# Longer load times in a kernel's own planner: the second batch's folds move back in GpSimd's order

## The chip, the cores and the metric

The kernel runs on one core of one Trainium2 chip. The metric is the device time of one execution in microseconds. A core has five engines that each work through their own instruction stream in order: TensorE (matmuls; PE in the profile, with its weight loads as PEld), VectorE (DVE), ScalarE (ACT), GpSimd (POOL) and SyncE (SP), which here only issues DMAs.

## The reference

A Fourier mixing step on 8 batches of 3008 rows with 256 columns, of which the real part is kept, and then a SwiGLU feed-forward layer on all 24064 rows:

```python
X = np.fft.fft(x, axis=1); X = np.fft.fft(X, axis=2)     # x: 8 x 3008 x 256
x = X.real.astype(np.float32).reshape(24064, 256)
g = x @ w_gate                                           # w_gate, w_val: 256 x 1536
val = x @ w_val
out = (g / (1 + np.exp(-g))) * val @ w_out               # w_out: 1536 x 256
```

## The kernel before

**The work.** The transform along the rows is a product with cosine and sine tables, and symmetry lets one half of the output rows carry the other (their mirror image). The transform along the columns is folded into the weights. The output columns of the eight half transforms, 8 times 1504, are cut into 24 tiles: 480 + 512 + 512 for the first batch, the same for the second, and 512 from there on. A tile has twelve units, one for each block of 128 hidden features; units are counted through all tiles, so unit 33 is the tenth of the third tile.

**A unit.** TensorE makes the gate `g` and the value `v` from the tile's even part `Pt` and odd part `Qt` (all at L1346). ScalarE and VectorE turn them into the gated product of the row, `hp` (L1560), and into the two factors of the mirror row, `sv` (ScalarE at L1533, VectorE at L1549). A buffer of `sv` holds the factors of two units, and there are two such buffers. GpSimd multiplies the factors of a pair of units: `hm` (L1557), 1024 elements in a partition. In some units GpSimd also makes `hp` (L1566), from a copy `pp` of the value (ScalarE, L1563). Until `hm` of a pair is done its `sv` buffer isn't free, and the pair after the next cannot be written. A tile later TensorE multiplies `hp` and `hm` with `w_out` (`o`, L1608), ScalarE evicts `ev`, and SyncE stores it (L1620).

**The folds.** Before the row transform of a batch, its rows are loaded (tile `XA` for the greater part, `XC` for the rest) and folded on GpSimd into sums and differences. One fold is six steps: `cross` (L189, L190), `even` (L193), `odd` (L196), `ab` (L199), `ce` (L202, L203) and `bb` (L211 to L213). The first step waits for all loads of its tile. The second batch has one fold of `XC` (into `Fc`, which SyncE spreads into `St`, L1735) and two folds of `XA` (into `CEa` and `BBa`). Small copies on GpSimd put one column of these aside (`Z`, L1877 and L1879). From `CEa`, `St` and `Z` TensorE makes the transform (`o` and `g`, L1766 and L605); ScalarE copies `od` out (L1773), and VectorE writes `Pt` and `Qt` with sums and differences (`puts`, L1783 and L1789). `sel` (L1937) is the first matmul of a tile that reads its `Qt`.

**The order.** All this is not written out in order. A planner in the kernel (class `Sched`) is told of each operation: its engine, a duration, what it reads and writes, and a due time, the plan's TensorE time plus a shift that a table gives for its kind and tile. `run` then deals the operations out greedily: for each engine it looks in a window of due times for the one that can begin first, and the engine's stream gets the order that comes out. Durations are guesses that set this order and nothing else: each instruction on the chip still waits for what it truly needs. A load has two numbers: `us`, how long SyncE is taken by it, and `ring`, how much later it lands than the load before. In `run`:

```python
if o.eng == "SP":
    ring = max(o.end + o.lat, ring + o.ring)
    o.lat = ring - o.end
    lanes = lanes[1:] + [ring]
```

With `lanes` no load starts until the eighth before it has landed. The loads of the second batch are listed in `run_loads` (L1669 on): `("C", 1)` are those of `XC`, 25 of them, and `("A", 1)` those of `XA`, 20, in the orders `C1_ORDER` and `A1_ORDER`, where `u` stands for blocks of rising rows and the other letters for sets of falling rows and a copy. `S.run({...})` at L2006 begins the plan; its numbers say how long after TensorE each engine is first free.

Of the kernel before, what the change touches and what calls it, by code (L numbers as in the profile page):

```python
# [31 lines left out]
def kernel(  # L32
# [113 lines left out]
    C1_ORDER = "uuduuduuduuduumuueuueuece"  # L146
    A1_ORDER = "uuuuduuuuduuuuduuuud"
# [1200 lines left out]
    S = Sched()  # L1348
# [307 lines left out]
    for b in range(2, B, 2):  # L1656
        u = slot[(b, 0)] - 1
# [11 lines left out]
    def run_loads(n):  # L1669
        for what, k, fn in loads[:n]:  # L1670
            up = k < (NA if what[0] == "A" else NC_)
            r, w, us, ring = [], [((what[0],), k)], 0.4 if up else 0.62, 0.57 if up or what[0] == "C" else 1.14
            if what == ("A", 1):
                r = [(("C",), C1_ORDER.rindex("u"))]
                us, ring = (0.35, 0.5) if A1_ORDER[k] == "u" else (0.65, 0.9)
            if what == ("C", 1):
                us, ring = (0.35, 0.45) if C1_ORDER[k] == "u" else (0.85, 0.75)
                if C1_ORDER[k] == "c":
                    r = [(("C",), j) for j, o in enumerate(C1_ORDER) if o == "u"]
            S.add("SP", us, fn, r=r, w=w, after=[(("A",), "pre" if A1_ORDER[k] == "d" else "preW")] if what == ("A", 1) else [],  # L1680
                  lat=2.5, ring=ring)
        del loads[:n]
# [4 lines left out]
    def fold_step(what, i, unit):  # L1687
        kind, b = what
        q, j = (1, i) if what == ("C", 1) else divmod(i, 6)
        if i == 0:  # L1690
            run_loads(max((k + 1 for k, (w_, _, _) in enumerate(loads) if w_ == what), default=0))
# [105 lines left out]
    for b, part in jobs[1:]:  # L1797
        for eo in range(2):
            u = slot[(b, part)] + eo
# [156 lines left out]
    for i, u in enumerate(units):  # L1956
# [6 lines left out]
        if i == A1_LOAD:  # L1963
            loads[0:0] = ((("A", 1), k, fn) for k, fn in enumerate(load_a(1, nc.sync)))
        run_loads(LOADS if i < 20 else LOADS_LATER)
        if i in ROW_PE:
            row_op(ROW_PE[i])
# [35 lines left out]
    part_b(prev)  # L2003
    owork = OWork(prev[0], ((psG, "g"), (psV, "v"), (psO, "o")))
    owork.run(len(owork.steps))
    S.run({'DVE': 1.2, 'ACT': 0.9, 'POOL': 3.5, 'PE': 0.0, 'SP': 1.0})  # L2006


# [28 lines left out]
```

## Time and profile before

| | |
|---|---|
| median of 3 runs | 607.98 us (607.45 to 609.18) |
| the profiled execution | 607.87 us |
| its span, from the first to the last instruction | 606.1 us |
| mean granted TensorE clock | 0.997 |
| GpSimd busy | 509.7 us, 460 instructions |
| VectorE busy | 571.4 us, 1055 instructions |
| ScalarE busy | 562.8 us, 1086 instructions |

A row of the timeline gives the start, the length, the engine, the line, the operation, the written and the read tile, and how many instructions were merged; in square brackets stands how long the engine had been idle and what ended that. A row of the windows gives for each engine the busy time and, in brackets, how many instructions, then the granted clock of TensorE (1.00 is full speed), the DMA engines' busy share and GB/s.

### The profile page before, as it was taken

To read this page: it belongs to the slowest core of one execution; us is meant where nothing else is said; L and a number is where in the kernel's file an instruction comes from. 1 tells how busy PE (TensorE), PEld (TensorE's weight loads), DVE (VectorE), ACT (ScalarE), POOL (GpSimd) and SP (SyncE) were. 2 spreads that over 40 slices of the span, in tenths; PEclk is the share of its full clock that TensorE was granted. 3 is DMA by queue.
4 is the path that set the end of the run, shared out by engine and by line. 5 is a ranking of instruction groups with operands and counts; after the bars stand their busy time and mean duration, and the time that the engine had idled before them with its cause. 6 is when DMAs were issued, how large, how long until landed. Compare 5 with 4: busy or idle time off the path is not lost.

```text
span 606.1 us, 12508 instructions
## 1 busy us (share of the span) xinstructions
PE 592.5 (98%) x3974; PEld 392.2 (65%) x4031; DVE 571.4 (94%) x1055; ACT 562.8 (93%) x1086; POOL 509.7 (84%) x460
## 2 busy tenths in 40 slices
PE   8999899999999999999999999999999999999997
PEld 5556566666666666666666666666666666666685
DVE  8989699999999999999999999999999999999993
ACT  8999798899989899999999999999999999999994
POOL 9737998999799999998999988887878467687772
PEclk9999899999999999999999999999999999999999
DMA  9846347254616214454136212036211112111112
GB/s 240 142 106 136 113 118 182 65 141 114 185 39 166 80 55 121 121 130 129 55 82 142 66 45 81 18 94 179 63 62 37 57 43 66 42 54 51 54 53 79
DMA packets 50555, 57.65 MB, mean 95 GB/s; under 512 B 7267, under 2 KB 37399, under 8 KB 50489
## 3 DMA queue, kind: packets, MB, share of 16 engines
q1 hardware_dynamic: 47529, 53.97, 32.8%
q0 software_dynamic: 2672, 2.36, 2.7%
q8 instruction: 31, 0.51, 0.4%
q10 hardware_dynamic: 288, 0.52, 0.3%
q14 instruction: 35, 0.29, 0.2%
HBM read 29.43 MB, written 24.65 MB: 89 GB/s over the span
## 4 chain that ended last, share of the span: by engine, by line
PE 88%; DMA 5%; ACT 2%; issue 1%; DVE 1%; POOL 1%; SPq 1%; DVEq 0%; ACTq 0%
PE o L1608 38%; PE g L1346 24%; PE v L1346 19%; DMA XA<-in_x_dram 3%; DMA XC<-in_x_dram 2%; PE g L1766 2%; PE o L1766 2%; PE v L1608 1%; PE o L1814 0%; POOL SDf L189 0%; ACT sp L1458 0%; PE o L605 0%; PE g L605 0%; POOL hm L1557 0%; ACT sv L1533 0%
## 5 line engine op out<-in xcount | busy, mean ns | idle before, releaser
L1557 POOL TENSOR_TENSOR hm<-sv 128x1024 bf16<-128x1024 f32 (+2 forms) x137 | 254.8, 1861 | 52.2 <-ACT sv L1533 24.0
L1549 DVE SCALAR_TENSOR_TENSOR sv<-es,v 128x512 f32<-128x512 f32 (+2 forms) x264 | 175.8, 670 | 9.3 <-PE v L1346 4.8
L1608 PE MATMUL o<-Wo,hm 128*128 128x256 bf16 (+1 forms) x1128 | 164.8, 274 | 0.4
L1560 DVE TENSOR_TENSOR hp<-sp,v 128x512 bf16<-128x512 f32 (+2 forms) x238 | 157.9, 670 | 5.0 <-PE v L1346 3.6
L1608 PE MATMUL o<-Wo,hp 128*128 128x256 bf16 (+1 forms) x1104 | 160.2, 272 | 0.7
L1608 PEld LDWEIGHTS <-hm 128*128 128x128 bf16 (+2 forms) x1140 | 112.6, 99 | 59.6 <-issue 3.3
L1608 PEld LDWEIGHTS <-hp 128*128 128x128 bf16 (+2 forms) x1140 | 111.9, 98 | 56.0 <-issue 1.8
L1533 ACT ACTIVATE sv<-g 128x512 f32<-128x512 f32 (+2 forms) x182 | 120.8, 678 | 5.6 <-POOL hm L1557 2.8
L1458 ACT ACTIVATE sp<-g 128x512 f32<-128x512 f32 (+2 forms) x182 | 113.5, 626 | 5.9 <-PE g L1346 3.2
L1346 PE MATMUL g<-Pt,Wp 128*128 128x512 bf16 (+2 forms) x282 | 105.8, 375 | 3.7 <-ACT sv L1533 2.7
L1419 ACT ACTIVATE v<-bc,w 128x512 f32<-128x512 bf16 (+2 forms) x146 | 105.4, 724 | 2.0 <-DVE sv L1549 1.0
L1346 PE MATMUL v<-Pt,Wp 128*128 128x512 bf16 (+2 forms) x287 | 105.3, 375 | 0.5
L1483 DVE SCALAR_TENSOR_TENSOR es<-bc,w,v 128x512 f32<-128x512 bf16 (+2 forms) x128 | 93.3, 732 | 2.7 <-PE v L1346 0.4
L1481 ACT ACTIVATE es<-v 128x512 f32<-128x512 f32 (+2 forms) x146 | 90.5, 622 | 5.6 <-DVE sv L1549 2.7
L1346 PE MATMUL g<-Qt,Wq 128*128 128x512 bf16 (+2 forms) x246 | 90.3, 374 | 0.3
L1346 PE MATMUL g<-Qt,Wm 128*128 128x512 bf16 (+2 forms) x192 | 72.1, 377 | 0.9 <-ACT sg L1381 0.5
L1346 PEld LDWEIGHTS <-Wp 128*128 128x128 bf16 x576 | 56.4, 98 | 25.1 <-issue 0.8
L1462 DVE SCALAR_TENSOR_TENSOR sg<-bc,w,g 128x512 f32<-128x512 bf16 (+2 forms) x92 | 66.2, 722 | 1.9 <-PE g L1346 1.5
L1533 ACT ACTIVATE sv<-sg 128x512 f32<-128x512 f32 (+2 forms) x92 | 64.0, 699 | 1.0 <-DVE sg L1526 0.9
L1530 ACT ACTIVATE sp<-g 128x512 f32<-128x512 f32 (+2 forms) x92 | 56.9, 618 | 5.3 <-DVE sg L1526 5.1
L1346 PEld LDWEIGHTS <-Wq 128*128 128x128 bf16 x430 | 42.0, 98 | 30.4 <-issue 6.4
L1526 DVE SCALAR_TENSOR_TENSOR sg<-sg,g 128x512 f32<-128x512 f32 (+2 forms) x92 | 60.7, 660 | 0.1
(196 smaller groups left out, 768.8 us busy)
## 6 DMA issues: line engine op xcount, KB each, us to landing
out_dram<-ev SPq DMA_DIRECT2D x96, 128.0 KB
XA<-in_x_dram SPq DMA_DIRECT2D x30, 256.0 KB
XA<-in_x_dram SPq DMA_DIRECT2D x112, 64.0 KB
XC<-in_x_dram SPq DMA_DIRECT2D x28, 120.0 KB
XC<-in_x_dram SPq DMA_DIRECT2D x105, 32.0 KB
bc<-br SPq DMA_DIRECT2D x19, 128.0 KB
St<-Fc SPq DMA_DIRECT2D x12, 128.5 KB
out_dram<-ev SPq DMA_DIRECT2D x12, 120.0 KB
```

What stands on the lines that cost most here:

```text
L1346: nc.tensor.matmul(ps[:, :n], Wt[:, gv, fs], src[:, :n], start=start, stop=stop, skip_group_check=True)
L1419: nc.scalar.activation(T_[kv][:, :w], bc[t][:, :w], AF.Copy, scale=w0[:, 1, f:f + 1])
L1458: nc.scalar.activation(sp_to()[:, :w], T_[kg][:, :w], AF.Silu)
L1462: nc.vector.scalar_tensor_tensor(T_[keg][:, :w], bc[t][:, :w], w0[:, 0, f:f + 1], T_[kg][:, :w], op0=Alu.mult, op1=Alu.add)
L1481: nc.scalar.activation(T_[kes][:, :w], T_[kv][:, :w], AF.Copy, scale=2.0 if on_pool(u) > 1 else 1.0)
L1483: nc.vector.scalar_tensor_tensor(T_[kes][:, :w], bc[t][:, :w], w0[:, 1, f:f + 1], T_[kv][:, :w], op0=Alu.mult, op1=Alu.add)
L1526: nc.vector.scalar_tensor_tensor(T_[kgm][:, :w], T_[keg][:, :w], 2.0, T_[kg][:, :w], op0=Alu.mult, op1=Alu.subtract)
L1533: nc.scalar.activation(sv()[:, f % 2, w - 1::-1, 1], T_[kgm if by_dve else kg][:, :w], AF.Silu)
L1549: nc.vector.scalar_tensor_tensor(sv()[:, f % 2, w - 1::-1, 0], T_[kes][:, :w], 2.0, T_[kv][:, :w], op0=Alu.mult, op1=Alu.subtract)
L1557: nc.gpsimd.tensor_tensor(hts_(t)[1][:, f - 1:f + 1, :w], sv()[:, :, :w, 1], sv()[:, :, :w, 0], op=Alu.mult)
L1560: nc.vector.tensor_tensor(hts_(t)[0][:, f, :wp], T_[ksp][:, :wp], T_[kv][:, :wp], op=Alu.mult)
L1608: nc.tensor.matmul(st["ps"][:n, j, :], hts[t][minus][:, f, c:c + n], Wo[:, f, :], start=(f == 0), stop=(f == nF - 1))
```

## The change

Two lines of planned load times and the line that begins the plan:

```diff
             if what == ("A", 1):
                 r = [(("C",), C1_ORDER.rindex("u"))]
-                us, ring = (0.35, 0.5) if A1_ORDER[k] == "u" else (0.65, 0.9)
+                us, ring = (0.35, 0.65) if A1_ORDER[k] == "u" else (0.65, 1.0)
             if what == ("C", 1):
-                us, ring = (0.35, 0.45) if C1_ORDER[k] == "u" else (0.85, 0.75)
+                us, ring = (0.45, 0.66) if C1_ORDER[k] == "u" else (0.9, 0.92)
...
-    S.run({'DVE': 1.2, 'ACT': 0.9, 'POOL': 3.5, 'PE': 0.0, 'SP': 1.0})
+    S.run({'DVE': 1.6, 'ACT': 1.2, 'POOL': 3.3, 'PE': 0.0, 'SP': 1.0})
```

No instruction is added, removed or changed; what comes out is another order. Around the fold of `XC` and the first fold of `XA`, GpSimd's order was and becomes (in parentheses the units of the second tile, counted from 0):

```
before                            after
XC: cross even odd ab bb ce       XC: cross even odd ab bb
hm (0,1)                          hp (1)
hp (1)                            hm (0,1)
XA: cross even odd                XC: ce
hm (4,5)                          hm (4,5)
hm (6,7)                          XA: cross
XA: ab bb ce                      hm (6,7)
hm (8,9)                          XA: even odd
hm (10,11)                        hm (8,9)
XA second fold: cross even        hm (10,11)
hm (third tile: 0,1)              XA: ab bb ce
...                               hm (third tile: 0,1)
                                  XA second fold: cross
```

Through this stretch the order of ScalarE, VectorE and TensorE is the same in both. They differ in two places: in the first tiles (some table builds and weight copies change places, `Wo`'s load comes one instruction earlier on GpSimd), and from the second batch's transform on, whose products stand 25 matmuls of 256 or 512 columns later in TensorE's order, its first `puts` three instructions later in VectorE's. On SyncE three stores of the first tile move ahead of eight loads of the next `XC`. From the fifth tile on the orders differ only by a few exchanged neighbours, and from the eleventh tile on not at all.

## The prediction

> **What bounds the kernel now.** First the page's busy times, then the windows of 20 us around the second batch's folds (columns: stretch, its length, busy PE, PEld, DVE, ACT, POOL, PEclk, DMA share, GB/s):
>
> ```profile
> span 606.1 us, 12508 instructions
> PE 592.5 (98%) x3974; PEld 392.2 (65%) x4031; DVE 571.4 (94%) x1055; ACT 562.8 (93%) x1086; POOL 509.7 (84%) x460
> ```
>
> ```profile
> 40.00:60.00 20.00, 19.86 (x128) 12.69 (x128) 19.38 (x33) 18.32 (x35) 12.77 (x13) 1.00 0.65 133
> 60.00:80.00 20.00, 17.17 (x106) 11.48 (x107) 15.02 (x25) 16.15 (x32) 19.92 (x19) 0.91 0.40 111
> 80.00:100.00 20.00, 19.89 (x136) 13.14 (x137) 20.00 (x42) 17.86 (x35) 17.00 (x17) 1.00 0.62 144
> ```
>
> TensorE is the bound: whatever makes it wait or run slowly is lost, and nothing else counts. Only 13.6 us of the span are left for that. The window from 60 us on sticks out: 17.17 us busy, 106 instructions against 128 and 136 in the windows beside it, and a clock of 0.91. So I read GpSimd's timeline there; ahead of it stands TensorE's longest wait of the whole run, from the view of waits (total, times, longest).
>
> ```profile
> PE g L1346 <- ACT sv L1533: 2.7, 1, 2.7
> ```
>
> ```profile
> 50.09 0.20 POOL L213 TENSOR_TENSOR Fc<-EOf 128x2 bf16<-128x2 f32 x1
> 50.84 0.64 POOL L203 TENSOR_TENSOR Fc<-Af 128x258 bf16<-128x258 f32 x1
> 51.44 1.89 POOL L1557 TENSOR_TENSOR hm<-sv 128x1024 bf16<-128x1024 f32 x1
> 53.29 1.28 POOL L1566 TENSOR_TENSOR hp<-sp,pp 128x512 bf16<-128x512 f32 x1
> 58.59 2.35 POOL L189 TENSOR_TENSOR SDf<-XA 128x1020 f32<-128x1020 f32 x1 [4.03 <-DMA XC<-in_x_dram]
> 63.16 3.74 POOL L1557 TENSOR_TENSOR hm<-sv 128x1024 bf16<-128x1024 f32 x2
> 66.86 1.10 POOL L199 TENSOR_TENSOR Af<-EOf 128x516 f32<-128x516 f32 x1
> 70.58 3.75 POOL L1557 TENSOR_TENSOR hm<-sv 128x1024 bf16<-128x1024 f32 x2
> ```
>
> GpSimd stands idle for 4.03 us at the head of the first `XA` fold, because the rows have not landed, and two `hm` of the second tile (units 4,5 and 6,7) stand behind the fold's first 4.57 us. Who waits for them:
>
> ```profile
> 56.74 0.68 ACT L1533 ACTIVATE sv<-g 128x512 f32<-128x512 f32 x1
> 65.08 0.64 ACT L1533 ACTIVATE sv<-g 128x512 f32<-128x512 f32 x1 [2.84 <-POOL hm L1557]
> 68.57 0.64 ACT L1533 ACTIVATE sv<-g 128x512 f32<-128x512 f32 x1
> 65.08 0.69 DVE L1549 SCALAR_TENSOR_TENSOR sv<-es,v 128x512 f32<-128x512 f32 x1 [3.74 <-POOL hm L1557]
> 62.51 0.60 PE L1608 MATMUL o<-Wo,hm 128*128 128x256 bf16 x4
> 65.77 0.38 PE L1346 MATMUL g<-Pt,Wp 128*128 128x512 bf16 x1 [2.67 <-ACT sv L1533]
> 65.98 0.38 PE L1346 MATMUL g<-Qt,Wq 128*128 128x512 bf16 x1
> ```
>
> Both `sv` buffers are full until the `hm` of units 4,5 ends at 63.16 + 1.87 = 65.03. At 65.08 ScalarE and VectorE go on with unit 8, and 0.7 us later TensorE, which had a gate buffer held by it. After that the clock falls:
>
> ```profile
> 65.77:70.27 4.50, 4.44 (x18) 2.90 (x18) 4.01 (x8) 3.80 (x7) 4.42 (x7) 0.62 0.49 139
> 70.27:74.77 4.50, 4.50 (x32) 3.03 (x31) 4.34 (x8) 4.30 (x9) 4.50 (x4) 1.00 0.39 104
> ```
>
> 18 matmuls in 4.50 us at a granted clock of 0.62, where the next 4.50 us hold 32.
>
> **Part 1: the stall goes.** In the changed order TensorE, ScalarE and VectorE do the same in the same order through this stretch; GpSimd alone is rearranged: `hp`, `hm` (0,1) and the `hm` of (4,5) come ahead of the `XA` fold, and `hm` (6,7) after its `cross`. I walk GpSimd with the rows' lengths:
>
> ```profile
> 50.37 0.56 ACT L1563 COPY pp<-v 128x512 f32<-128x512 f32 x1
> 53.16 0.54 SPq L153 DMA_DIRECT2D XA<-in_x_dram  x1
> 53.81 4.76 SPq L166 DMA_DIRECT2D XC<-in_x_dram  x8
> ```
>
> The `XC` fold starts when its loads land, as before. `hp` now stands at 50.29 and waits for `pp` (50.93), so 51.0 to 52.3; `hm` (0,1) to 54.1; `ce` (1.25) to 55.4. `hm` (4,5) waits for the `sv` of unit 5, which ScalarE ends at 56.74 + 0.68 = 57.42: 57.45 to 59.32. That frees its buffer 5.7 us earlier than before. The `XA` rows land at 58.59 at the latest. Their last load is issued at 53.16, and nothing ahead of it on SyncE moves; behind it three stores of 256 KB together replace eight loads of as much. So `cross` runs 59.32 to 61.8 without a wait, `hm` (6,7) to 63.7. Unit 8 wants its buffer at 62.2, when ScalarE is free (65.08 less 2.84), and has it 2.9 us before. Unit 10 followed unit 8 by 3.49 us (68.57, half of it at the low clock); at full pace it wants the other buffer some 2.5 to 3.5 us after 62.2, a microsecond or two after 63.7. No wait is left.
>
> What this gives: TensorE's gap, from 62.51 + 0.44 (four products of 256 columns at half of the 0.216 us between 65.77 and 65.98 each, 0.109) = 62.95 to 65.77, is 2.82 us. The slow stretch holds 6 matmuls of 512 columns and 12 of 256: 6 x 0.216 + 12 x 0.109 = 2.60 us at full clock, against 4.50, so 1.90 more. Gross gain 4.72 us. A cross-check: 106 instructions instead of some 132 (the mean of the neighbours) at 0.15 us each is 3.9 us.
>
> [...]
>
> **Part 2: what comes next late.** GpSimd regains less than TensorE, for it still loses time: 0.7 us at `hp` and 2.1 us before `hm` (4,5). From 57.45 on it does in a row what it did from 58.59 on, so it is 1.1 us ahead, while the others are 4.7 ahead. The places where it is read next:
>
> ```profile
> 84.36 0.63 POOL L203 TENSOR_TENSOR CEa<-Af 128x258 bf16<-128x258 f32 x1
> 88.25 0.20 POOL L1879 COPY Z<-CEa 128x4 bf16<-128x4 bf16 x1
> 89.04 1.89 POOL L1557 TENSOR_TENSOR hm<-sv 128x1024 bf16<-128x1024 f32 x1 [0.59 <-ACT sv L1533]
> 93.27 1.89 POOL L1557 TENSOR_TENSOR hm<-sv 128x1024 bf16<-128x1024 f32 x1 [2.33 <-DVE sv L1549]
> 95.12 2.36 POOL L189 TENSOR_TENSOR SDf<-XC 128x1020 f32<-128x1020 f32 x1
> 87.63 0.33 PE L1766 MATMUL g<-Tab,CEa 128*128 128x189 bf16 x2
> 90.99 0.49 PE L605 MATMUL o<-Tab,Z 128*128 128x189 bf16 x3
> 94.58 0.37 PE L1937 MATMUL g<-Qt,sel 128*128 128x480 bf16 x1
> 91.76 0.51 ACT L1773 COPY od<-o 128x377 f32<-128x377 f32 x1
> 93.04 1.19 DVE L1783 TENSOR_TENSOR Qt<-g,od 128x188 bf16<-128x188 f32 x5
> 94.15 0.15 DVE L1789 TENSOR_TENSOR Qt<-g,od 128x1 bf16<-128x1 f32 x1
> 84.16 0.63 SPq L168 DMA_DIRECT2D XC<-in_x_dram  x1
> ```
>
> *`CEa`.* Before it was done at 84.99, after 26.40 us of GpSimd without a pause since 58.59. Now one more `hm` (units 4,5 of the third tile, 1.87) stands ahead: 57.45 + 26.40 + 1.87 = 85.7. TensorE's first product with it now has 5 matmuls of 512 and 20 of 256 columns more ahead, 3.26 us: 87.63 + 3.26 - 4.72 = 86.2. Reached with 0.5 us to spare. `Z` is ready 1.6 us after `CEa` (`bb`, which is 88.25 less 84.99 less the `hm` between them, 1.4, and the copy, 0.20), at 87.3, and TensorE wants it 1.6 us after its first product (a `g` and five matmuls), at 87.8. Reached with 0.5. Cost 0; if GpSimd is late by more, up to 0.7 us.
>
> *The third tile's end to the fourth tile's `Qt`.* The last transform product now is an `o`, after which the ScalarE copy (0.51) and six `puts` (1.26) are due before `sel`; with three handoffs of some 0.2 us (an estimate, from the 0.28 us between the last `put`, which ends at 94.30, and `sel` at 94.58) that is 2.4 us. Behind that `o` TensorE has 7 matmuls of about 512 columns and 8 of 256, 2.36 us. No margin: 0 if both engines are free at that moment, up to 1.4 us if each has one instruction of 0.7 us ahead. I take 0.4.
>
> *The `sv` buffers of the third and fourth tile.* GpSimd frees them. It idled for 0.59 and 2.33 us ahead of 89.04 and 93.27; that it can take up, which makes it 1.1 + 2.9 = 4.0 us ahead from there on at best, the others 4.3. Where the margin was smaller than the difference, a bit is lost: 0 to 0.6, taken as 0.2.
>
> *The first 45 us.* Table builds and copies change places.
>
> ```profile
> 34.62 0.51 ACT L1895 ACTIVATE St<-EOf,sgn 128x256 bf16<-128x256 bf16 x1
> 35.52 0.48 PE L1766 MATMUL o<-Tab,BBa 128*128 128x376 bf16 x2
> ```
>
> The copy at 34.62 (0.51) stood behind the last sine table and now stands ahead of it, and the first product that reads the tables came 0.9 us after the sine's end. Between the sine and that product VectorE still scales the table. So 0.1, from -0.3 to 0.4.
>
> *The next `XC` fold.* It comes forward to 95.12 - 4.0 = 91.1. The last load in front is issued by 84.79; the last `XA` load took 58.59 - 53.70 = 4.89 us from its issue, so 89.7. Hidden by 1.4 us.
>
> Behind that all orders are alike up to a few neighbours, and every load waits for a fold or store that comes as much earlier. Sum: 4.72 - 0.4 - 0.2 - 0.1 = 4.0 us. Against the profiled execution, 607.87 (its span 606.1 and 1.77 around it), that is 603.9; that execution lies 0.1 below the median of the three runs, 607.98.
>
> **The rivals.**
>
> *GpSimd stays the bound* (0.16). Its lead, 1.1 growing to 4.0 us, rather than TensorE's 4.7 sets the pace from 60 to 125 us, and `CEa`, `sel` and a buffer each cost their upper bound: 4.72 - 0.7 - 1.4 - 0.6 = 2.0, with the first 45 us 1.6 to 2.3. Time 605.9. For it: GpSimd was 19.92 us busy of 20 from 60 us on. Against: it idles 3 us at 80 to 100 us, where it can catch up.
>
> *The slow clock has another cause* (0.06). Then the 4.50 us at 0.62 come without the gap too, and the gain is 2.82 - 0.7 = 2.1, time 605.8. [...]
>
> *The wait moves to another load* (0.08, slower than before). GpSimd meets the next `XC` fold earlier. If the rows land after 95 us, the fold holds up GpSimd with `hm` (10,11) of the third tile behind, just as the `XA` fold did. A wait of 6 us there would cost TensorE some 4.8 us and 1.9 us of half clock: 6.7 - 4.0 = 2.7 slower, 610.6. It decides from a landing 10 us after the issue on, against the 4.89 us seen: unlikely.
>
> *It doesn't do what it says* (0.08). The `XA` rows land later with the stores behind them or the first stage shifts, and a stall of nearly the same size stays: 607.0, from 606.3 to 607.9.
>
> **How the numbers follow.** The forecast (603.9; 603.0 to 605.0 by its bounds) has 0.62. Differences of 0.3%, 1.8 us, are about what a measurement of this kernel can tell from no change. Faster by more than that (below 606.1): forecast 0.62, and two thirds of the two smaller gains, 0.15; together 0.77. Same: the rest of these and the last rival, 0.15. Slower: 0.08. The range takes in the smaller gains: 602.8 to 606.4.
>
> **What would show it.** In the changed profile, GpSimd's first `XA` `cross` should have no DMA wait or less than 0.5 us, and stand behind three `hm`/`hp` of the second tile; the waits of ScalarE and VectorE for `hm` should be gone, the window from 60 to 80 us should hold some 132 TensorE instructions at a clock of 1.00, and the windows after 100 us should be as before, 4 us earlier. It would be wrong if TensorE showed a wait of over a microsecond at `CEa` or `sel`, if the clock fell again anywhere, or if a fold waited for rows.

## The result and the profile after

The changed kernel takes 603.47 us (median of 6 runs, 603.0 to 603.94), against 607.87 for the kernel before in runs beside it (6 runs, 607.45 to 609.8). The ratio is 0.9921, with a 95% interval of 0.9905 to 0.9936: faster by 4.4 us. The profiled execution took 603.29 us, 1.8 of it around the span.

The busy times of the page, and the same three windows as before (busy PE, PEld, DVE, ACT, POOL, then PEclk, DMA share, GB/s):

```profile
span 601.5 us, 12495 instructions
PE 590.3 (98%) x3974; PEld 390.5 (65%) x4031; DVE 572.5 (95%) x1055; ACT 562.5 (94%) x1086; POOL 510.1 (85%) x460
```

```profile
40.00:60.00 20.00, 19.86 (x129) 12.78 (x129) 19.39 (x34) 18.33 (x34) 13.70 (x14) 1.00 0.65 140
60.00:80.00 20.00, 19.84 (x135) 13.39 (x137) 19.54 (x32) 20.00 (x41) 19.92 (x18) 1.00 0.40 107
80.00:100.00 20.00, 19.95 (x140) 13.29 (x139) 19.57 (x42) 16.16 (x32) 19.82 (x20) 1.00 0.62 157
```

The middle window has gone from 106 TensorE instructions to 135 and from a clock of 0.91 to 1.00. GpSimd is as busy there as it was, 19.92 us, but in the third window it has 19.82 instead of 17.00: it does the same work sooner. Its timeline through the changed stretch:

```profile
51.22 1.27 POOL L1566 TENSOR_TENSOR hp<-sp,pp 128x512 bf16<-128x512 f32 x1 [0.51 <-PE v L1346]
52.45 1.89 POOL L1557 TENSOR_TENSOR hm<-sv 128x1024 bf16<-128x1024 f32 x1
54.91 0.64 POOL L203 TENSOR_TENSOR Fc<-Af 128x258 bf16<-128x258 f32 x1
57.72 1.89 POOL L1557 TENSOR_TENSOR hm<-sv 128x1024 bf16<-128x1024 f32 x1 [2.18 <-ACT sv L1533]
59.57 2.36 POOL L189 TENSOR_TENSOR SDf<-XA 128x1020 f32<-128x1020 f32 x1
62.04 1.90 POOL L1557 TENSOR_TENSOR hm<-sv 128x1024 bf16<-128x1024 f32 x1
65.98 3.75 POOL L1557 TENSOR_TENSOR hm<-sv 128x1024 bf16<-128x1024 f32 x2
...
85.32 0.64 POOL L203 TENSOR_TENSOR CEa<-Af 128x258 bf16<-128x258 f32 x1
87.37 0.20 POOL L1879 COPY Z<-CEa 128x4 bf16<-128x4 bf16 x1
91.22 2.35 POOL L189 TENSOR_TENSOR SDf<-XC 128x1020 f32<-128x1020 f32 x1
```

The `XA` cross at 59.57 has no bracket: GpSimd spends the time until the rows land on the `hm` of units 4,5 and waits for nothing afterwards. Units 8 and 10 find their `sv` buffers free (ScalarE's timeline, no brackets):

```profile
62.34 0.64 ACT L1533 ACTIVATE sv<-g 128x512 f32<-128x512 f32 x1
65.29 0.71 ACT L1533 ACTIVATE sv<-g 128x512 f32<-128x512 f32 x1
```

TensorE reaches the three places that the prediction feared without a bracket, here in its timeline, and its longest waits of the whole run are now elsewhere (view of waits); all four were there in before, where the one for the first `XA` rows was 0.6 us shorter:

```profile
86.47 0.33 PE L1766 MATMUL o<-Tab,CEa 128*128 128x189 bf16 x2
88.10 0.49 PE L605 MATMUL g<-Tab,Z 128*128 128x189 bf16 x3
91.44 0.37 PE L1937 MATMUL g<-Qt,sel 128*128 128x480 bf16 x1
```

```profile
PE o L310 <- DVE sel L261: 1.0, 1, 1.0
PE v L497 <- ACT EOb L512: 1.0, 2, 0.8
PE g L444 <- DMA XA<-in_x_dram: 0.8, 1, 0.8
PE g L1346 <- ACT sp L1530: 0.7, 1, 0.7
```

**Where the time comes from** is seen when TensorE's timelines of the two kernels are laid side by side, matmul by matmul: the start in before less the start after is TensorE's lead. One place serves as an example, the gate product behind the slow stretch, first of before, then of after:

```profile
70.27 0.38 PE L1346 MATMUL g<-Qt,Wm 128*128 128x512 bf16 x1
```

```profile
65.76 0.38 PE L1346 MATMUL g<-Qt,Wm 128*128 128x512 bf16 x1
```

The lead is -0.21 us up to before's 62.51, 4.51 at 70.27, 4.40 still at 150, 4.59 at 168, 4.38 at 590. The whole gain, 4.72 us, arises within 8 us, and little of it is given back.

### The profile page after: what moved, and what is told of

Its sections match the earlier page's. It is cut to its first block, busy times and chain, and to the rows that moved or that the text cites. A ratio compares the mean times of both kernels' runs of the same rounds, so it can differ in the third digit from the quotient of the medians.

```text
span 601.5 us, 12495 instructions
## 1 busy us (share of the span) xinstructions
PE 590.3 (98%) x3974; PEld 390.5 (65%) x4031; DVE 572.5 (95%) x1055; ACT 562.5 (94%) x1086; POOL 510.1 (85%) x460
## 4 chain that ended last, share of the span: by engine, by line
PE 90%; ACT 3%; DVE 2%; issue 2%; DMA 2%; POOL 1%; SPq 0%; ACTq 0%; DVEq 0%
PE o L1608 39%; PE g L1346 24%; PE v L1346 20%; PE g L1766 2%; PE o L1766 2%; DMA XA<-in_x_dram 1%; PE v L1608 1%; DVE sv L1549 1%; ACT sp L1458 1%; ACT sv L1533 1%; PE o L1814 1%; POOL EOA L511 0%; ACT v L1419 0%; PE g L605 0%; DVE es L1483 0%
## 5 line engine op out<-in xcount | busy, mean ns | idle before, releaser
L1346 PE MATMUL v<-Qt,Wm 128*128 128x512 bf16 (+2 forms) x158 | 59.0, 374 | 0.6
```

Source lines behind the costliest of these rows:

```text
L1346: nc.tensor.matmul(ps[:, :n], Wt[:, gv, fs], src[:, :n], start=start, stop=stop, skip_group_check=True)
```

## Experiments

Two theories. Theory 1: GpSimd has no time to spare from 58 to 88 us, so the stall is only where its lateness first shows; take it away there, and it comes back at the next place that needs GpSimd. Theory 2: the one wait for rows, with the `hm` behind it, is everything.

Experiments 1 to 4 take the kernel before and move operations in GpSimd's stream alone, after the planning. All other engines keep before's order. Their edit is a helper that is called in `run`'s last loop:

```diff
+def rearranged(order):
+    pool = [o for o in order if o.eng == "POOL"]
+    for move, at, after in (((15, 16, 17), 18, 1),):
+        move, at = [pool[k] for k in move], pool[at]
+        order = [o for o in order if o not in move]
+        i = order.index(at) + after
+        order[i:i] = move
+    return order
...
-            for o in order:
+            for o in rearranged(order):
```

The numbers count GpSimd's operations in before's order: 15, 16, 17 are `cross`, `even` and `odd` of the first `XA` fold, 18 and 19 the `hm` of units 4,5 and 6,7, 20 to 22 the fold's last three steps, 24 the `hm` of units 10,11; from 25 on follow the second `XA` fold and the third tile's `hm`. The lead columns of the table below are worked out as above, from rows of the timelines.

**Experiment 1, e1_hm_first**: `((15, 16, 17), 18, 1)`, the fold's first three steps behind the `hm` of units 4,5.

> The kernel before with one exchange on GpSimd: the hm of units 4,5 of the second tile ahead of the first three steps of the XA fold (cross, even, odd); all other engines keep their order. Theory 1 (GpSimd has no time to spare from 58 to 88 us: every hm there frees an sv buffer that is wanted at once, and the folds stand between them): the stall at unit 8 goes, but GpSimd is only 1.1 us ahead of before (57.45 instead of 58.59), so new waits of ScalarE and VectorE for hm come up at the third tile's units 0, 6 and 8, where before there was 0.9, 0.5 and 0.05 us of margin. Gain 1.1 to 1.2 us, 606.7. Theory 2 (one stall, behind one wait for rows, is all there is): the whole gain, 603.5.

607.25 us, ratio 0.9982 [0.9974, 0.9991]. TensorE's timeline, and two lines of its waits view (50 to 130 us):

```profile
65.87 0.38 PE L1346 MATMUL g<-Qt,Wm 128*128 128x512 bf16 x1
...
67.42 0.38 PE L1346 MATMUL v<-Pt,Wp 128*128 128x512 bf16 x1 [0.52 <-ACT v L1419]
73.13 0.38 PE L1346 MATMUL g<-Qt,Wq 128*128 128x512 bf16 x1 [0.22 <-DVE sg L1462]
74.23 0.38 PE L1346 MATMUL g<-Pt,Wp 128*128 128x512 bf16 x1 [0.52 <-ACT sv L1533]
84.20 0.38 PE L1346 MATMUL g<-Qt,Wm 128*128 128x512 bf16 x1 [0.74 <-ACT sp L1458]
88.24 0.38 PE L1346 MATMUL g<-Pt,Wp 128*128 128x512 bf16 x1 [0.40 <-ACT sv L1533]
...
93.80 0.37 PE L1937 MATMUL g<-Qt,sel 128*128 128x480 bf16 x1
```

```profile
DVE sv L1549 <- POOL hm L1557: 2.4, 2, 1.8
ACT sv L1533 <- POOL hm L1557: 2.4, 3, 1.1
```

The big wait and the low clock are gone, and at the product that begins at 70.27 in before TensorE leads by 4.40. Then five waits, each for ScalarE or VectorE, whose own longest waits are for `hm`, take most of it back: 2.4 us in the brackets, and some 0.16 more at each, as a row of 0.38 us ends later than the next product can begin (0.22 us on). With smaller gaps that no bracket shows, the lead at `sel` is 0.78. Theory 2 falls.

**Experiment 2, e2_one_step**: `((16, 17), 18, 1)`, only `even` and `odd` behind that `hm`; `cross` with its wait stays in front.

> The kernel before with the hm of units 4,5 of the second tile behind the first step (cross) of the XA fold instead of behind three; GpSimd still waits for the rows at 58.59. Theory 1: the stall at unit 8 shrinks from 2.8 us to some 0.8 and the clock stays at 1.00 there, but GpSimd's work up to 88 us ends when it did before, and the third tile's unit 8, whose buffer came free 0.05 us before it was wanted, now waits for it: gain 0.0 to 0.3 us, 607.7. Theory 2: the stall is shorter by 2.1 us and the half clock (1.9) gone: gain 4.0, 603.9. For the clock: if a gap of under a microsecond leaves it at 1.00, the 2.82 us were what lowered it.

607.75 us, 0.9990 [0.9981, 0.9999]. The row wait of 3.64 us is still there, but the clock never falls (1.00 in every window); TensorE's lead at 70.27 is 3.88, and 0.27 at `sel`. So before's wait for rows costs little by itself: nearly the same wait, with one step instead of three between it and the `hm`, gives 4.17 of the 4.72 at first and loses most of it likewise. Experiment 1, which has no such wait, ends 0.5 us sooner.

**Experiment 3, e3_stretch**: `((15,), 18, 1), ((16, 17), 19, 1), ((20, 21, 22), 24, 1)`, the changed kernel's order on GpSimd up to the first fold's end.

> The kernel before with GpSimd's order of the changed kernel in the second tile alone: hm 4,5, cross, hm 6,7, even, odd, hm 8,9, hm 10,11, ab, bb, ce; from the second XA fold on as before, and all other engines as before. Theory 1: no wait within the second tile, but in the third, where the fold's steps still stand ahead of hm as before and GpSimd is 1.1 us ahead only: gain 1.2 us, 606.7. Theory 2: 603.5.

607.32 us, 0.9983 [0.9974, 0.9992]. The windows and the later of TensorE's waits:

```profile
60.00:80.00 20.00, 20.00 (x136) 13.37 (x135) 19.53 (x32) 19.14 (x39) 19.92 (x19) 1.00 0.40 113
80.00:100.00 20.00, 17.10 (x116) 11.01 (x115) 16.92 (x37) 15.16 (x30) 17.03 (x17) 1.00 0.58 156
```

```profile
80.62 0.38 PE L1346 MATMUL g<-Qt,Wm 128*128 128x512 bf16 x1 [0.55 <-ACT sp L1458]
84.67 0.38 PE L1346 MATMUL g<-Qt,Wm 128*128 128x512 bf16 x1 [1.94 <-ACT sp L1458]
88.72 0.38 PE L1346 MATMUL g<-Pt,Wp 128*128 128x512 bf16 x1 [0.42 <-ACT sv L1533]
```

Here the first 20 us are without any loss, TensorE busy for 20.00 of 20.00, and the second 20 have it instead. The stall has moved to the third tile's `sv` buffers, behind the second `XA` fold, which is still where it was.

**Experiment 4, e4_gpsimd_all**: experiment 3 and `((25,), 27, 1), ((26, 28), 31, 1), ((30, 29, 32, 33), 34, 1)`, so that GpSimd has the changed kernel's order through the second fold too. TensorE's transform stays where it was.

> The kernel before with GpSimd's order of the changed kernel from the XA fold to the end of the third tile's folds; TensorE, ScalarE and VectorE keep the order of before, in which the second batch's transform stands 25 matmuls earlier. Theory 1: no sv wait, but CEa is ready at 86.0 and TensorE wants it at 83.2: a TensorE wait of up to 2.8 us at L1766, which may halve the clock once more (1.9 us): gain 0 to 1.7, 606.2 to 607.9. Theory 2 (GpSimd's order is all that matters): 603.5.

608.09 us, 0.9994 [0.9985, 1.0004]: no gain at all. TensorE's timeline:

```profile
85.43 0.26 PE L1766 MATMUL g<-Tab,CEa 128*128 128x189 bf16 x1 [2.01 <-POOL CEa L202]
86.03 0.26 PE L1766 MATMUL g<-Tab,CEa 128*128 128x188 bf16 x1 [0.34 <-POOL CEa L203]
```

Now no `sv` buffer is late, and `CEa` is: it is written at 84.74 and 85.34, where before's TensorE, 4.5 us ahead, wants it from 83.4 on. Behind this gap the clock falls again, to 0.50 from 86.80 to 90.00 us (last section). The four runs in one table:

| lead over before, us | TensorE at 62.51 | at 70.27 | at `sel`, 94.58 | GpSimd at `Z`, 88.25 |
|---|---|---|---|---|
| e2_one_step | -0.29 | 3.88 | 0.27 | 0.27 |
| e1_hm_first | -0.32 | 4.40 | 0.78 | 0.79 |
| e3_stretch | -0.79 | 3.94 | 0.30 | 0.31 |
| e4_gpsimd_all | -0.25 | 4.47 | 0.00 | 0.87 |

The first column is what the first 60 us happened to differ by. From it to the second column, each but e2 gains 4.72 or 4.73. By `sel` TensorE's lead has shrunk, in three of four to GpSimd's own within 0.01 us; over the stretch, experiments 1 and 3 keep 1.1 us, which is the 1.1 that the prediction's walk gave GpSimd. In the fourth, `CEa` comes later in GpSimd's order and takes the rest as well.

**Experiment 5, e5_loads_only**, and **6, e6_begin_only**: the change without its third line, and that line alone.

```diff
 # e6_begin_only; e5_loads_only is the other two lines
-    S.run({'DVE': 1.2, 'ACT': 0.9, 'POOL': 3.5, 'PE': 0.0, 'SP': 1.0})
+    S.run({'DVE': 1.6, 'ACT': 1.2, 'POOL': 3.3, 'PE': 0.0, 'SP': 1.0})
```

> The change without its last line: the longer load times, with the plan begun as before. The order of the first tiles is then that of before, and all the rest that of the changed kernel. Theory 1: the whole gain, 603.5. Rival (the exchanges in the first tiles matter): 0.3 us or more beside 603.5.

> The last line of the change alone: the plan begun with other times. Only the first tiles' order changes (table builds, weight copies, one load). Theory 1: nothing, 607.9, within 0.3. Rival: up to a microsecond either way.

The loads alone give 602.51 us, 0.9911 [0.9897, 0.9925]: all of the gain. The last line alone gives 607.26, 0.9986 [0.9978, 0.9995], 0.8 us that I had not expected. GpSimd's and TensorE's timelines show the old stall, smaller:

```profile
57.95 2.36 POOL L189 TENSOR_TENSOR SDf<-XA 128x1020 f32<-128x1020 f32 x1 [3.50 <-DMA XC<-in_x_dram]
65.14 0.38 PE L1346 MATMUL g<-Pt,Wp 128*128 128x512 bf16 x1 [1.98 <-ACT sv L1533]
```

The rows landed 0.64 us earlier than in before (57.95 against 58.59), `Z` comes 0.66 earlier (87.59) and `sel` 0.64 (93.94). Again GpSimd's lead is TensorE's. Why the rows landed earlier I did not test. Whether it adds anything to the change was the next question.

**Experiments 9, e9_change_again, and 10, e10_loads_again**: the change and experiment 5, side by side.

> The changed kernel once more, for a comparison on one chip with the next one: 0.9921 of before, 603.3. Theory 1 as it stands: the first tiles' order is worth nothing in the changed kernel, so this and the next are equal within 0.3 us. Rival: the next is faster by 0.6 us or more, and the change's last line costs that.

> The longer load times without the change's last line, beside the changed kernel on one chip. Theory 1: equal within 0.3 us. Rival: faster by 0.6 us or more (602.5 against 603.5, as the medians of two different chips stand).

603.29 us, 0.9924 [0.9911, 0.9938], and 603.02, 0.9921 [0.9908, 0.9935]. The two can't be told apart: the third line does nothing for the changed kernel that these runs show, and none of them points to a version that beats it.

**Experiments 11, e11_xa_only, and 12, e12_xc_only**: one of the two load lines each.

```diff
 # e11_xa_only
-                us, ring = (0.35, 0.5) if A1_ORDER[k] == "u" else (0.65, 0.9)
+                us, ring = (0.35, 0.65) if A1_ORDER[k] == "u" else (0.65, 1.0)
 # e12_xc_only
-                us, ring = (0.35, 0.45) if C1_ORDER[k] == "u" else (0.85, 0.75)
+                us, ring = (0.45, 0.66) if C1_ORDER[k] == "u" else (0.9, 0.92)
```

> The longer times for the XA loads alone. In GpSimd's order cross and even of the XA fold then still stand ahead of the hm of units 4,5. Theory 1: the stall at unit 8 shrinks to 1.8 us, and GpSimd's work up to 88 us ends when it did before: gain 0.0 to 0.6, 607.5. Theory 2 (later folds are better, by as much as they are later): half the gain, 605.8.

> The longer times for the XC loads alone. cross of the XA fold stands ahead of the hm of units 4,5. Theory 1: a stall of 0.8 us at unit 8, GpSimd at most 0.4 us ahead of before at 88 us: gain 0.3 to 0.9, 607.3. Theory 2: half the gain or more, 605.8 or less.

`XA` alone: 607.65 us, 0.9997 [0.9988, 1.0006]. TensorE waits at both of the places that experiments 1 to 4 separated, at the second tile's gate and in the third tile:

```profile
64.83 0.38 PE L1346 MATMUL g<-Pt,Wp 128*128 128x512 bf16 x1 [1.13 <-ACT sv L1533]
85.21 0.38 PE L1346 MATMUL g<-Qt,Wm 128*128 128x512 bf16 x1 [1.45 <-ACT sp L1458]
```

`XC` alone: 608.69, 1.0014 [1.0005, 1.0023], a miss, for I had expected a small gain. Up to 135 us it has one: the lead goes from -0.93 at 62.51 to 1.03. It is lost after that, in a tile that this order arranges otherwise; the window from 140 us on, of this kernel and of after:

```profile
140.00:160.00 20.00, 17.59 (x112) 10.50 (x113) 16.73 (x34) 18.20 (x37) 18.52 (x18) 1.00 0.54 130
```

```profile
140.00:160.00 20.00, 19.13 (x126) 12.27 (x128) 18.60 (x39) 20.00 (x40) 17.64 (x18) 1.00 0.55 144
```

At 160 us the lead is -2.05. A load time that is told to the planner moves everything behind it, not only what it was meant for; here that costs 3 us, 80 us later.

**Experiment 7, e7_cross_first**: the changed kernel, with one step set back, `((16,), 15, 0)` (numbers of the changed order): the `XA` cross again ahead of the `hm` of units 4,5.

> The changed kernel with one exchange: the XA fold's cross ahead of the hm of units 4,5 again, so that GpSimd waits for the rows first. Theory 1: unit 8 waits 0.8 us for its buffer, GpSimd is 1.1 us later from there on, TensorE waits some 0.5 us at CEa, where the changed kernel has 0.5 us of margin, and loses 0.7 to 1.2 us in all: 604.2 to 604.7. Theory 2 (the wait for the rows is the cause): the gain goes back to a half or less, 605.5 or more.

603.97 us, 0.9936 [0.9923, 0.9948]. GpSimd waits for the rows again:

```profile
57.69 2.36 POOL L189 TENSOR_TENSOR SDf<-XA 128x1020 f32<-128x1020 f32 x1 [2.54 <-DMA XA<-in_x_dram]
```

VectorE then waits 0.9 us for an `hm`. TensorE has no wait that the view shows singly, only small gaps from 62 to 68 us; against after it is 0.38 us ahead at 54 and 0.27 behind at 102, so the step costs 0.65 us. A wait of 2.54 us on GpSimd that costs 0.65: theory 1's figure nearly (the rows landed 0.9 us earlier than in before), and far from a return of the 4.4.

**Experiment 8, e8_six_steps**: before, with the stall made longer, `((20, 21, 22), 18, 0)`: all six steps of the fold ahead of the `hm` of units 4,5.

> The kernel before with the hm of units 4,5 of the second tile behind all six steps of the first XA fold: GpSimd frees the buffer 3.72 us later. Both theories: TensorE's gap grows from 2.8 to 6.5 us, time 611.6. For the clock: if the half clock after the gap lasts as long as it did behind 2.82 us (3.4 us), its price is fixed once it falls; if it grows with the gap, more than 612.

612.28 us, 1.0074 [1.0059, 1.0088]. TensorE's timeline:

```profile
68.81 0.59 PE L1346 MATMUL g<-Pt,Wp 128*128 128x512 bf16 x1 [5.52 <-ACT sv L1533]
```

The wait grows from 2.67 to 5.52 us, and the time at half clock from 3.4 to 6.8 us, of which matmuls run for 5.3 (last section). What is placed ahead of that `hm` is paid for at TensorE, in full and more.

## Why the prediction was right

**The bound and the stall.** The gross term, 2.82 us of gap and 1.90 of half clock, 4.72, is what TensorE gains in after, in experiment 1 and in experiment 3 between before's 62.51 and 70.27 (4.51 + 0.21, 4.40 + 0.32, 3.94 + 0.79). But the half clock is a loss of the profiled execution rather than of the kernel. Of the 21 executions of before beside experiments 9 to 12, nine have a mean clock of 0.997 or less, as one such fall makes it (3.4 us at 0.50 in a span of 606.1), and take 608.09 us on average; the other twelve have 0.998 or more, too high for a fall, and take 607.92. Beside experiments 1 to 8 the difference is 0.3 to 0.4 us, not 1.9. No trace of an execution of before without the fall was kept, but experiment 2 shows where the time can go: there the clock stays up, and what TensorE gains is lost in waiting further on. The changed kernel has neither the fall nor those waits, so the sum held.

**The walk** holds to 0.3 us: `hm` (4,5) at 57.72 (said: 57.45), the cross at 59.57 (59.32) without a wait, `hm` (6,7) done at 63.94 (63.7), unit 8 at 62.34 (wanted at 62.2), unit 10 at 65.29.

**What comes next late.** `CEa` is done at 85.96 and wanted at 86.47 (said: 85.7 and 86.2), `Z` at 87.57 and 88.10 (87.3 and 87.8). The margin is the half microsecond that was forecast, and experiment 4 shows what it hangs on: without the 3.26 us of matmuls that the change puts ahead of the transform on TensorE, the same order on GpSimd is worth nothing. The next `XC` fold begins at 91.22 (91.1), with no wait for rows.

**What was mis-sized** are the small terms. For `sel` 0.4 and for the `sv` buffers 0.2 were taken; the lead falls from 4.51 to 4.40 by 150 us, so both together cost 0.1. The first 45 us, taken at 0.1, cost 0.2 in the profiled execution (the lead of -0.21); in the paired runs the line that rearranges them made no difference. Behind 150 us the lead drifts, 4.59 at 168 and 4.38 at 590, and the spans differ by 4.6 in the end, where the prediction had 4.0; these last 0.2 us either way I did not trace.

**The rivals.** *GpSimd stays the bound* didn't happen, but it is the one that the experiments speak of most: it is exactly what happens when only GpSimd's order is changed (1 to 4), and I had given its weight to `sel` and a buffer rather than seen that the 3.26 us decide it. *The slow clock has another cause* falls: in before and in experiments 4, 6 and 8 the clock falls at TensorE's longest gap (2.67, 2.01, 1.98 and 5.52 us), within 1.2 us of its end or, in experiment 8, inside it, wherever that gap is, and nowhere else from 40 to 100 us. *The wait moves to another load* and *it doesn't do what it says* have no row for them.

**Shown and not shown.** Shown: that the order on GpSimd alone yields 0 to 1.1 us, that the transform's place on TensorE makes up the rest, since experiment 4 and after differ in the second batch's stretch by that, by what follows from it on the other engines, and by two exchanges that no wait of TensorE's points to (three stores on SyncE, and `ce`, `hm` and `hp` behind the `XC` fold), and that both load lines are needed and the third isn't. Not shown: why GpSimd can begin on the rows at 57.7 in some executions and only at 58.6 or later in others, and TensorE's new order without GpSimd's, which was not run.

## What to carry to other kernels

When the longest wait is for an engine that is itself busy 99% of that stretch, removing the wait is worth only the lead that this engine gains; lay the two traces side by side and compare its lead with the bound's. Then look for the other half: what the bound asks of it next has to move back too, and here a planner that was told longer load times moved both together. Run each planned time by itself, since a better figure in one place can rearrange a tile 80 us later for the worse.

## What the runs showed of the hardware

The granted clock falls once between 40 and 100 us in the traces of before, e4_gpsimd_all, e6_begin_only and e8_six_steps. Here are the windows around each fall, in this order (columns: stretch, length, busy PE, clock, DMA share, GB/s):

```profile
65.77:66.60 0.83, 0.77 (x3) 0.94 0.61 149
66.60:69.80 3.20, 3.20 (x13) 0.50 0.44 136
69.80:71.00 1.20, 1.20 (x10) 0.95 0.47 110
```

```profile
85.40:86.80 1.40, 1.02 (x7) 0.94 0.60 187
86.80:90.00 3.20, 3.20 (x13) 0.50 0.53 99
90.00:92.00 2.00, 2.00 (x17) 0.99 0.64 120
```

```profile
65.20:66.40 1.20, 1.15 (x7) 0.93 0.46 140
66.40:69.70 3.30, 3.30 (x14) 0.51 0.47 138
69.70:71.00 1.30, 1.30 (x10) 1.00 0.44 101
```

```profile
67.00:67.70 0.70, 0.00 (x0) 0.78 0.28 105
67.70:68.80 1.10, 0.00 (x0) 0.50 0.52 170
68.80:74.10 5.30, 5.29 (x19) 0.50 0.41 105
74.10:76.00 1.90, 1.90 (x13) 0.97 0.21 70
```

The last two columns of the table are worked out from these rows: a row's length, times what its clock lacks of 1.00, over 0.50, is its time at half clock.

| | TensorE's longest gap, us | its end | the clock falls | time at half clock, us |
|---|---|---|---|---|
| before | 2.67 | 65.77 | 66.5 | 3.4 |
| e4_gpsimd_all | 2.01 | 85.43 | 86.6 | 3.4 |
| e6_begin_only | 1.98 | 65.14 | 66.2 | 3.4 |
| e8_six_steps | 5.52 | 68.81 | 67.4 | 6.8 |

In the first three, TensorE is still at full clock for 0.7, 1.2 and 1.1 us behind the gap before the clock falls. In experiment 8 the clock falls 4.1 us into the gap, and matmuls run for 5.3 of the 6.8 us at half clock. The gap of 1.94 us in e3_stretch leaves the clock at 1.00 from 80 to 100 us.

Not shown: what decides whether the clock falls behind a gap (twelve of the 21 executions of before beside experiments 9 to 12 have a mean clock too high for a fall, and none of them has a trace), and why the half clock lasts twice as long in experiment 8.
